# An FFT-mixing and three-way maxout kernel on one core: one more split unit per batch, x in two transfers instead of four, indexed stores moved, the last column of the head fetched through DRAM

## The chip, the cores and the metric

The kernel runs on one core of one Trainium2 chip. The metric is the device time in microseconds (us). The kernel before takes 392.08 us, the median of three runs (391.94 to 392.52). A difference of about 0.2%, 0.8 us, is what such a measurement can tell from no change.

## The reference

Two stages follow each other, all inputs and outputs in float32:

```python
# x: (8, 3072, 256);  w1, w2, w3: (256, 768);  w_out: (768, 256)
X = np.fft.fft(x, axis=1)
X = np.fft.fft(X, axis=2)
t = X.real.reshape(8 * 3072, 256)
h = np.maximum(np.maximum(t @ w1, t @ w2), t @ w3)
out = h @ w_out
```

## The kernel before

Each engine has one instruction stream, written in the order in which the Python code records the operations (`manual_schedule`). The work of one batch of x has two parts.

**Mixing.** x of a batch is fetched into `xt[b % 2]`: 96 rows apart lie on one partition, 32 partitions hold them in order (`h == 0`), 32 more hold their mirror images (`h == 1`), which is read backwards, row by row. `load_x` (L116) issues these transfers from GpSimd (POOL in the profile). `mirror`/`turn` (L123, L785) copy the upper 64 partitions from the lower ones with the columns reversed; from batch 2 on ScalarE (ACT) does it, eight pieces a batch (`turn`, units 5 to 12 two batches ahead). `s` (L392) multiplies with a 64-column table and evicts into `tb`; batch 0 turns `tb` with a VectorE (DVE) transpose (`t`, L428), later batches go through DRAM (`y`, `z`). `k` (L456) gives the cosine and sine sums `tE` and `tO` (512 columns a block, three blocks); row 0 of `tO` goes to DRAM (`vd`) and back to all partitions (`vb`, `v`, L468).

**The maxout layer.** The second FFT is folded into the weights: `g_all` holds w2 and w3 minus w1, times cosines and sines; `gd_all` is what turns the sum `tE, tO` (row block "plus") into the difference ("minus"). A batch is 18 units: unit u treats block u // 6 and hidden chunk u % 6, 512 tokens wide, plus and minus. A plain unit has six 512-column matmuls on TensorE (PE): four in `unit_plus` and two in `unit_minus`, and `unit_out` (L495) takes the maximum with one ACT and one DVE operation for each of plus and minus. A **split** unit has five: `third(g)` (L837) makes `e3` and `d3`, ACT makes `odd3`, DVE makes `even3` with the column `wcol`, and POOL adds and subtracts them (`plus3`, `minus3`, L850), two units ahead of use; `begin` (L852) and `finish` (L869) then need two matmuls plus one. All odd units from unit 7 on are split, and the even ones named in `EXTRA` (`EXTRA_LAST` in the last batch), from batch 1 on: 91 units of 144.

**The second layer.** `l2_block` (L553) multiplies `hp`, `hm` with `wout_bf`; `l2_some(10)` (L905) lets ten of its matmuls run in each unit. Plain rows are stored from SyncE (SP); the mirrored rows wait in `waiting` until `scatter(n)` (L649) issues n indexed stores from POOL, five a batch: one in units 8, 10 and 12 and two in unit 14 (L904).

What a unit's loop body (L880 to L917) records, in order: `begin(g)`, `finish(g-1)`, `third(g+2)`, `scatter`, ten matmuls of the second layer, and then the pieces that `plan` (L754) has for the unit: pieces of the next batch's mixing, transfers of x (`fetch`, L781; four a batch), and in batch 0 the rest of the preparation: `prep_first` (`next(first)`), `column` (L345, 24 one-column matmuls that make `wcol`), `prep_second`, `rows` (L727, the index column of the indexed stores, on POOL).

**The head** (L147 to L725) stands before the units: the first x in four pieces (`FIRST`, L147), ramps on POOL, tables on ACT and DVE, weights, `m.t()`, the first `k`. In the last batch `flipped` (L889) copies `tE` and `tO` backwards on POOL at unit 12, and `l2_last` (L584) ends the kernel.

Of the kernel before, what the change touches and what calls it, by code (L numbers as in the profile page):

```python
# [9 lines left out]
FP32 = mybir.dt.float32  # L10
BF16 = mybir.dt.bfloat16
# [16 lines left out]


FIRST_OF = (4, 8, 1)  # L30
EXTRA, EXTRA_LAST = (0, 4, 8), (0, 4, 8, 14)


def _parts(g):
# [10 lines left out]
def kernel(  # L45
# [9 lines left out]
    nc = tc.nc  # L55

    B, S, D = x.shape
    assert (S, D) == (3072, 256)
    DFF = moe_w1.shape[1]
    NJC = DFF // 128  # L60
# [3 lines left out]
    NS = 49  # L64
# [6 lines left out]
    consts = ctx.enter_context(tc.tile_pool(name="consts", bufs=1))  # L71
    ps_f = ctx.enter_context(tc.tile_pool(name="ps_f", bufs=3, space=bass.MemoryType.PSUM))
    d_pool = ctx.enter_context(tc.tile_pool(name="dbuf", bufs=1, space=bass.MemoryType.DRAM))
    dbs = [d_pool.tile([NS, 64 * 128], BF16, name=f"db{i}", tag=f"db{i}") for i in range(2)]
    vds = [d_pool.tile([1, NHALF], BF16, name=f"vd{i}", tag=f"vd{i}") for i in range(2)]
    t_pool = ctx.enter_context(tc.tile_pool(name="tbuf", bufs=2))

    xt = [consts.tile([128, NS * 256], BF16, name=f"xt{i}", tag=f"xt{i}") for i in range(2)]
# [17 lines left out]
    md = [md_all[:, fc * 256:(fc + 1) * 256] for fc in range(2)]  # L96
    nmd = [nmd_all[:, fc * 256:(fc + 1) * 256] for fc in range(2)]
    w1_bf = consts.tile([128, 2 * DFF], BF16, tag="w1_bf")
    w2_bf = consts.tile([128, 2 * DFF], BF16, tag="w2_bf")
    w3_bf = consts.tile([128, 2 * DFF], BF16, tag="w3_bf")  # L100
    wout_bf = consts.tile([128, NJC * 256], BF16, tag="wout_bf")
    g1t = consts.tile([128, NJC * 256], BF16, tag="g1t")
    g_all = consts.tile([128, 4 * DFF], BF16, tag="g_all")
# [6 lines left out]
    mark = consts.tile([1, 1], FP32, tag="mark")  # L110
    sgn = consts.tile([128, 1], FP32, tag="sgn")
    wcol = consts.tile([128, NJC], FP32, tag="wcol")
    dif = consts.tile([128, 1], FP32, tag="dif")
    t_mid = consts.tile([128, 2, B], BF16, tag="t_mid")

    def load_x(b, s0, s1, h):  # L116

        rows = x[b].rearrange("(a s) d -> a s d", s=96)
        lo, hi = (s0, s1) if h == 0 else (max(s0, 1), min(s1, 48))
        src = rows[:, lo:hi, :] if h == 0 else rows[:, 97 - hi:97 - lo, :][:, ::-1, :]  # L120
        return nc.gpsimd.dma_start(out=xt[b % 2][32 * h:32 * h + 32, lo:hi, :], in_=src)  # L121

    def mirror(b, s0, s1):  # L123

        t = xt[b % 2]
        fn = (nc.vector.tensor_copy, (nc.gpsimd.tensor_copy, nc.vector.tensor_copy)[s0 >= 25],
              nc.scalar.copy)[min(b, 2)]
        fn(out=t[64:128, s0:s1, 1:128], in_=t[0:64, s0:s1, 255:128:-1])  # L128
        if b < 2:
            if b == 0 and s0 < 40:  # L130
                fn = nc.scalar.copy
            fn(out=t[64:128, s0:s1, 0], in_=t[0:64, s0:s1, 128])
# [8 lines left out]
    ps_s = ps_s_cm.__enter__()  # L141

    def iota(t, pattern, base=0, cm=0):
        nc.gpsimd.iota(t, pattern, base=base, channel_multiplier=cm,
                       allow_small_or_imprecise_dtypes=True)

    FIRST = ((0, 16), (16, 32), (32, 40), (40, NS))  # L147

    pidx = gen.tile([128, 1], FP32, tag="pidx")
    iota(pidx, [[0, 1]], cm=1)  # L150
    pidx_i = gen.tile([128, 1], INT32, tag="pidx_i")
# [18 lines left out]
            iota(kvec[:, NHALF:NHALF + 1], [[0, 1]], base=0)  # L170

    dvec = gen.tile([128, 128], FP32, tag="dvec")
    for c, (s0, s1) in enumerate(FIRST):
        for h in range(2):
            load_x(0, s0, s1, h)
        if c == 0:
            iota(dvec, [[1, 128]])
        elif c < 3:
            ramp(c - 1)

    def load_w(k, j0, j1):
# [162 lines left out]

    def column():  # L345

        psc = ps_f.tile([128, 512], FP32, name="psc", tag="ps")
        for jc in range(NJC):
            for k, (table, wt) in enumerate(((md, w3_bf), (nmd, w1_bf))):
                for fc in range(2):  # L350
                    nc.tensor.matmul(psc[:, jc:jc + 1],
                                     wt[:, fc * DFF + jc * 128: fc * DFF + jc * 128 + 128],
                                     table[fc][:, 128:129],
                                     start=(k == 0 and fc == 0), stop=(k == 1 and fc == 1))
        nc.scalar.copy(out=wcol, in_=psc[:, 0:NJC])

    def prep_second():

# [290 lines left out]
    def scatter(n):  # L649

        for _ in range(min(n, len(waiting))):
            row, col, p0, p1, src = waiting.pop(0)
            stored(nc.gpsimd.indirect_dma_start(  # L653
                fours, bass.IndirectOffsetOnAxis(ap=rows_m[p0:p1, col:col + 1], axis=0),
                src, None, element_offset=256 * row), "scattered", ("scattered", "direct"))
            nc.gpsimd.memset(mark, 0.0)
# [11 lines left out]
    def warm_up(n):  # L668
        for _ in range(n):
            nc.tensor.matmul(warm, zero[:, 0:128], zero, start=True, stop=True)  # L670

    m = Mix(0)
# [8 lines left out]
    m.s(2, pool=ps_s)  # L681
    m.s(3, pool=ps_s)
    warm_up(1)
    mirror(0, *FIRST[3])
    m.s(4, pool=ps_s)
    warm_up(2)
    scal(sgn, pidx, 0.0, ALU.is_equal)
    scal(sgn, sgn, 2.0, ALU.mult, -1.0, ALU.add)
    scal(dif, sgn, 1.0, ALU.subtract)
    m.s(5, pool=ps_s, evict=dve)  # L690
    nc.scalar.activation(out=md_all, in_=vm, func=AX.Sin, scale=float(2.0 * math.pi / 256.0),
                         bias=turn[:, 0:1])
    m.s(6, pool=ps_s)
    m.t()
    warm_up(2)
# [20 lines left out]
    table(1, 512, 1024)  # L716
    m.c(1, 16)
    warm_up(1)
    m.k(0, 0, dve)
    m.k(1, 0)  # L720
    differ(0, 2, 0, 128)
    keep(psg2, 1, 2, 128, 384, dve)
    differ(0, 2, 128, 384)
# [32 lines left out]
    def at(b, unit, fn):  # L756
        plan.setdefault((b + unit // UNITS, unit % UNITS), []).append(fn)
# [23 lines left out]
    def fetch(b, k):  # L781
        half, h = divmod(k, 2)
        load_x(b, *HALVES[half], h)
# [4 lines left out]
    for (u, fn) in ((0, lambda: table(2, 512, 1024)),   # L788
                    (0, lambda: next(second)), (0, lambda: next(first)),
                    (1, lambda: m.k(1, 1)), (1, lambda: next(second)), (1, lambda: next(first)),  # L790
                    (1, lambda: table(0, 512, 1024)),
                    (2, lambda: m.v(1)), (2, lambda: m.k(0, 1)), (2, lambda: next(first)),
                    (2, lambda: next(second)), (2, lambda: next(first)), (2, lambda: table(1)),
                    (3, lambda: m.c(16, RI)), (3, lambda: m.c(0, 1)),
                    (3, lambda: table(2)), (3, lambda: table(0)),
                    (4, lambda: m.k(1, 2)), (4, lambda: m.k(0, 2)), (4, m.end),
                    (5, rows), (5, column), (5, lambda: next(second)), (6, lambda: m.v(2))):
        at(0, u, fn)

    for ch in range(4):  # L800
        at(0, (3, 3, 4, 4)[ch], lambda ch=ch: mirror(1, *CHUNKS[ch]))
        at(0, 4, lambda ch=ch: fetch(2, ch))
    for b in range(2, B):
        for ch in range(4):
            if b > 2:
                at(b - 3, (9 + (b == 3), 11, 18, 19)[ch], lambda b=b, ch=ch: fetch(b, ch))
        for ch in range(8):
            at(b - 2, 5 + ch + 3 * (b == 2), lambda b=b, ch=ch: turn(b, ch))
        at(b - 2, 13 + 3 * (b == 2), lambda b=b: mirror_first(b))
# [70 lines left out]
    for g in range(B * UNITS):  # L880
        b, u = divmod(g, UNITS)
        blk, jc = divmod(u, NJC)
        mm = mixes[b]
        last = b == B - 1 and blk == 2
        if jc == 0:
            hp = h_pool.tile([128, NJC, TOKB], BF16, name="hp", tag="hp")
            hm = h_pool.tile([128, NJC, TOKB], BF16, name="hm", tag="hm")
            if last:
                flipped = []  # L889
                for t, name in ((mm.tE, "tEr"), (mm.tO, "tOr")):  # L890
                    fl = h_pool.tile([128, TOKB], BF16, name=name, tag=name)
                    flipped.append(fl)
                    nc.gpsimd.tensor_copy(fl, t[:, 3 * TOKB - 1: 2 * TOKB - 1: -1])
        if prev is not None and is_split(prev[0]) and not is_split(g):
            finish(*prev)
            prev = None
        pses = begin(g, hp[:, jc, :])
        if prev is not None:
            finish(*prev)
        prev = (g, pses, hm[:, jc, ::-1] if last else hm[:, jc, :])  # L900
        for lead in (1, 2):
            if is_split(g + lead) and (lead == 1) == (g + lead == 7):
                third(g + lead)
        scatter({8: 1, 10: 1, 12: 1, 14: 2}.get(u, 0))  # L904
        l2_some(10)  # L905
        if b == B - 1 and u in (1, 3):
            if u == 1:
                middle = l2_mid()
            next(middle, None)
        for fn in plan.get((b, u), ()):  # L910
            fn()
        if jc == NJC - 1:
            l2_some(1000)
            if g == B * UNITS - 1:
                finish(*prev)
            l2_queue.append(l2_last(hp, hm, mm.tE, mm.tO, flipped) if last else
                            l2_block(b, blk, hp, hm, mm.tE, mm.tO))  # L917
# [32 lines left out]
```

## Time and profile before

| what | before |
|---|---|
| median of the runs | 392.08 us |
| the profiled execution | 391.42 us, span 389.3 us |
| PE busy | 376.2 us, 97% of the span |
| DVE, POOL, ACT busy | 84%, 81%, 64% |
| granted TensorE clock | 0.998 |
| DMA moved | 54.13 MB, 139 GB/s on average |

The span is the time from the first to the last instruction of the profiled execution; 2.1 us of its own time lie outside it. In an instruction's row the first two numbers are its start and length in us, and the brackets tell how long the engine was idle before it and what it waited for. A PE row of several matmuls overlaps with the next: the spacing of the starts is what a matmul costs. Rows with SPq are transfers that SP issues; their length is the time of the issue, not that of the transfer.

### The profile page before, as it was taken

How to read it: one execution, taken by the hardware profiler on the slowest of the kernel's cores; microseconds unless marked ns; L12 is line 12 of the kernel's file. 1: busy time of each engine (PE TensorE's matmuls, PEld its weight loads, DVE VectorE, ACT ScalarE, POOL GpSimd, SP SyncE). 2: the span in 40 equal slices, each digit the busy share in tenths (PEclk: the TensorE clock that was granted, in tenths of full speed). 3: DMA queues.
4: the chain of work that ended last, by engine and by line, in shares of the span. 5: the costliest groups of instructions: out<-in, count | busy, mean ns of one | idle time of the engine just before them, and what ended most of it. 6: DMA issues, size and time to landing. Idle time of an engine off the chain costs nothing.

```text
span 389.3 us, 8092 instructions
## 1 busy us (share of the span) xinstructions
PE 376.2 (97%) x2817; PEld 236.2 (61%) x2817; DVE 327.7 (84%) x552; ACT 248.4 (64%) x453; POOL 314.3 (81%) x363
## 2 busy tenths in 40 slices
PE   6699999999999999999999999999999999999985
PEld 2355566566665666566665666656665666666654
DVE  7788797799797988899797988989887997999972
ACT  6877789567856696567856687567866346434420
POOL 9983576879898898879898898879787887769881
PEclk9999999999999999999999999999999999999999
DMA  7999764585747666475938657575423544212226
GB/s 113 184 183 160 163 145 118 112 168 161 178 141 130 172 176 154 111 128 186 189 120 149 169 151 176 125 128 185 113 94 93 149 138 139 70 31 80 85 89 206
DMA packets 52263, 54.13 MB, mean 139 GB/s; under 512 B 26547, under 2 KB 45009, under 8 KB 51367
## 3 DMA queue, kind: packets, MB, share of 16 engines
q0 software_dynamic: 20272, 26.45, 34.4%
q1 hardware_dynamic: 31418, 26.58, 25.0%
q10 hardware_dynamic: 532, 0.59, 0.5%
q8 instruction: 22, 0.36, 0.3%
q14 instruction: 19, 0.16, 0.1%
HBM read 36.95 MB, written 30.81 MB: 174 GB/s over the span
## 4 chain that ended last, share of the span: by engine, by line
PE 87%; POOL 4%; DVE 4%; DMA 2%; ACT 1%; issue 1%; DVEq 0%; POOLq 0%
PE po L549 30%; PE pse L492 10%; PE pse L860 5%; PE pse L485 5%; PE pse L486 5%; PE d L843 5%; PE e L841 5%; PE pse L861 5%; PE po L572 5%; PE ps L461 3%; PE ps L396 3%; PE pl L565 2%; DMA xt<-in_x_dram 2%; POOL xt L121 1%; POOL plus L850 1%
## 5 line engine op out<-in xcount | busy, mean ns | idle before, releaser
L850 POOL TENSOR_TENSOR plus<-even,odd 128x512 bf16<-128x512 f32 x91 | 115.7, 1271 | 55.4 <-DVE even L846 44.1
L850 POOL TENSOR_TENSOR minus<-even,odd 128x512 bf16<-128x512 f32 x91 | 115.5, 1269 | 0.0
L845 ACT ACTIVATE odd<-d 128x512 f32<-128x512 f32 x91 | 54.4, 598 | 55.8 <-PE d L843 41.9
L862 DVE SCALAR_TENSOR_TENSOR hp<-pse,plus 128x512 bf16<-128x512 f32 x91 | 62.6, 688 | 32.2 <-PE pse L861 27.9
L549 PE MATMUL po<-wout_bf,hp 128*128 128x256 bf16 x576 | 86.1, 273 | 0.0
L498 ACT ACTIVATE stmp<-pse 128x512 bf16<-128x512 f32 x106 | 63.2, 600 | 24.2 <-PE pse L486 11.2
L549 PE MATMUL po<-wout_bf,hm 128*128 128x256 bf16 x576 | 78.6, 273 | 0.0
L549 PEld LDWEIGHTS <-hp 128*128 128x128 bf16 x576 | 56.3, 98 | 26.2
L492 PE MATMUL pse<-tO,gd_all 128*128 128x512 bf16 x197 | 66.1, 380 | 1.3 <-DVE hp L862 1.3
L846 DVE SCALAR_TENSOR_TENSOR even<-vb,wcol,e 128x512 f32<-128x512 bf16 x91 | 67.1, 737 | 0.0
L549 PEld LDWEIGHTS <-hm 128*128 128x128 bf16 x576 | 56.3, 98 | 16.4
L874 DVE SCALAR_TENSOR_TENSOR hm<-pse,minus 128x512 bf16<-128x512 f32 x91 | 61.9, 680 | 0.4
L499 DVE TENSOR_TENSOR hp<-pse,stmp 128x512 bf16<-128x512 f32 x53 | 36.4, 686 | 8.8 <-ACT stmp L498 4.2
L499 DVE TENSOR_TENSOR hm<-pse,stmp 128x512 bf16<-128x512 f32 x53 | 36.5, 689 | 6.7 <-ACT stmp L498 4.3
L485 PE MATMUL pse<-tE,g_all 128*128 128x512 bf16 x106 | 40.2, 379 | 0.8 <-DVE tE L463 0.4
L577 DVE TENSOR_TENSOR kq<-po,even 128x512 f32<-128x512 f32 x60 | 40.9, 682 | 0.0
L128 ACT COPY xt<-xt 64x762 bf16<-64x762 bf16 (+1 forms) x48 | 39.8, 838 | 1.0
L486 PE MATMUL pse<-tO,g_all 128*128 128x512 bf16 x106 | 40.2, 379 | 0.0
L572 PE MATMUL po<-gw,tO 128*128 128x512 bf16 x92 | 34.9, 379 | 0.0
L860 PE MATMUL pse<-tE,g_all 128*128 128x512 bf16 x91 | 34.6, 380 | 0.1
L653 POOL DMA_INDIRECT out_dram<-kq,rows_m x29 | 29.0, 1000 | 6.8 <-issue 5.7
L841 PE MATMUL e<-tE,g_all 128*128 128x512 bf16 x91 | 34.5, 379 | 0.0
(173 smaller groups left out, 511.7 us busy)
## 6 DMA issues: line engine op xcount, KB each, us to landing
xt<-in_x_dram POOLq DMA_DIRECT2D x14, 384.0 KB
db<-tb SPq DMA_DIRECT2D x21, 192.0 KB
out_dram<-obuf SPq DMA_DIRECT2D x8, 384.0 KB
out_dram<-kq SPq DMA_DIRECT2D x8, 384.0 KB
vb<-vd SPq DMA_DIRECT2D x23, 128.0 KB
xt<-in_x_dram POOLq DMA_DIRECT2D x7, 400.0 KB
xt<-in_x_dram POOLq DMA_DIRECT2D x7, 368.0 KB
out_dram<-kq SPq DMA_DIRECT2D x7, 288.0 KB
```

The costliest lines, as they stand in the source:

```text
L485: nc.tensor.matmul(pse[:, 0:n], g_all[:, jc, 2 * i, :], te, start=True, stop=False)
L486: nc.tensor.matmul(pse[:, 0:n], g_all[:, jc, 2 * i + 1, :], to, start=False, stop=True)
L492: nc.tensor.matmul(pse, gd_all[:, jc, i, :], to, start=False, stop=True, skip_group_check=True)
L498: nc.scalar.activation(out=stmp[:, 0:n], in_=pses[0][:, 0:n], func=AX.Relu)
L499: nc.vector.tensor_tensor(out=dst, in0=src3, in1=stmp[:, 0:n], op=ALU.max)
L549: nc.tensor.matmul(po, hcols(jc), wout_bf[:, jc * 256:(jc + 1) * 256], start=False, stop=(jc == NJC - 1), skip_group_check=True)
L572: nc.tensor.matmul(po, to[:, cp], gw[:, 256:768], start=True, stop=True)
L845: nc.scalar.activation(out=odd3, in_=d3, func=AX.Copy, scale=-0.5)
L846: nc.vector.scalar_tensor_tensor(out=even3, in0=vb, scalar=wcol[:, jc:jc + 1], in1=e3, op0=ALU.mult, op1=ALU.add)
L850: nc.gpsimd.tensor_tensor(out=dst, in0=even3, in1=odd3, op=op)
L862: nc.vector.scalar_tensor_tensor(out=dst, in0=pse2, scalar=0.0, in1=sums[g][0], op0=ALU.max, op1=ALU.max)
L874: nc.vector.scalar_tensor_tensor(out=dst, in0=pses[0], scalar=0.0, in1=sums.pop(g)[1], op0=ALU.max, op1=ALU.max)
```

## The change

- **Split units.** `EXTRA` gets unit 12; in the last batch unit 12 takes the place of unit 14.
- **Indexed stores.** One in units 0, 4, 8, 12 and 14, in the last batch also one in unit 16.
- **x.** From batch 3 on a batch comes in two transfers, `h == 0` at unit 13 and `h == 1` at unit 18 three batches ahead, instead of four at units 9 (10), 11, 18 and 19. Batches 0 to 2 keep theirs, but for the first.
- **The first x.** The transfer of its first 16 rows is issued before the first `iota`s on POOL; the last nine rows come as five and four.
- **Head evictions.** The evictions of `s(5)`, `k(0, 0)` and `k(1, 0)` are halved between DVE and ACT; `md_all` is made on ACT before the half of `s(5)`, and three small DVE operations (`sgn`, `dif`) go ahead of the last mirrors.
- **The column.** `wcol` is no longer computed: row 0 of `g_all[:, :, 3, :]` is written to DRAM from SP (unit 3), read back as a column of 2-byte elements (`column_read`, unit 4, SP), and cast on POOL (`column_done`, unit 5, ahead of `rows`).

```diff
-EXTRA, EXTRA_LAST = (0, 4, 8), (0, 4, 8, 14)
+PACE, PACE_LAST = {0: 1, 4: 1, 8: 1, 12: 1, 14: 1}, {0: 1, 4: 1, 8: 1, 12: 1, 14: 1, 16: 1}
+EXTRA, EXTRA_LAST = (0, 4, 8, 12), (0, 4, 8, 12)
...
+    wd = d_pool.tile([1, DFF], BF16, name="wd", tag="wd")
...
+    wcol_b = consts.tile([128, NJC], BF16, tag="wcol_b")
...
-    FIRST = ((0, 16), (16, 32), (32, 40), (40, NS))
+    FIRST = ((0, 16), (16, 32), (32, 40), (40, 45), (45, NS))
+    def load_first(c):
+        for h in range(2):
+            load_x(0, *FIRST[c], h)
+    load_first(0)
     pidx = gen.tile([128, 1], FP32, tag="pidx")
...
-    for c, (s0, s1) in enumerate(FIRST):
-        for h in range(2):
-            load_x(0, s0, s1, h)
-        if c == 0:
-            iota(dvec, [[1, 128]])
-        elif c < 3:
+    iota(dvec, [[1, 128]])
+    for c in range(1, 5):
+        load_first(c)
+        if c < 3:
             ramp(c - 1)
...
     def column():
-        psc = ps_f.tile([128, 512], FP32, name="psc", tag="ps")
...
-        nc.scalar.copy(out=wcol, in_=psc[:, 0:NJC])
+        nc.sync.dma_start(out=wd.rearrange("o (c j) -> o c j", j=128), in_=g_all[0:1, :, 3, :])
+    def column_read():
+        nc.sync.dma_start(out=wcol_b, in_=wd.rearrange("o (c j) -> j (o c)", j=128))
+    def column_done():
+        nc.gpsimd.tensor_copy(wcol, wcol_b)
...
     warm_up(1)
-    mirror(0, *FIRST[3])
-    m.s(4, pool=ps_s)
-    warm_up(2)
     scal(sgn, pidx, 0.0, ALU.is_equal)
...
-    m.s(5, pool=ps_s, evict=dve)
+    mirror(0, *FIRST[3])
+    mirror(0, *FIRST[4])
+    m.s(4, pool=ps_s)
+    warm_up(2)
     nc.scalar.activation(out=md_all, in_=vm, func=AX.Sin, scale=float(2.0 * math.pi / 256.0),
                          bias=turn[:, 0:1])
+    def halves(out, in_):
+        n = out.shape[-1] // 2
+        if len(out.shape) == 4:
+            n = 2
+            dve(out=out[:, :, 0:n, :], in_=in_[:, :, 0:n, :])
+            nc.scalar.copy(out=out[:, :, n:, :], in_=in_[:, :, n:, :])
+        else:
+            dve(out=out[:, 0:n], in_=in_[:, 0:n])
+            nc.scalar.copy(out=out[:, n:], in_=in_[:, n:])
+    m.s(5, pool=ps_s, evict=halves)
...
-    m.k(0, 0, dve)
-    m.k(1, 0)
+    m.k(0, 0, halves)
+    m.k(1, 0, halves)
...
-                    (5, rows), (5, column), (5, lambda: next(second)), (6, lambda: m.v(2))):
+                    (3, column), (4, column_read), (5, column_done), (5, rows), (5, lambda: next(second)), (6, lambda: m.v(2))):
...
-        for ch in range(4):
+        for h in range(2):
             if b > 2:
-                at(b - 3, (9 + (b == 3), 11, 18, 19)[ch], lambda b=b, ch=ch: fetch(b, ch))
+                at(b - 3, (13, 18)[h], lambda b=b, h=h: load_x(b, 0, NS, h))
...
-        scatter({8: 1, 10: 1, 12: 1, 14: 2}.get(u, 0))
+        scatter((PACE if b < B - 1 else PACE_LAST).get(u, 0))
```

More of the change, by code (lines that the diff above doesn't have):

```diff
@@ L345, in column @@
     def column():
-        psc = ps_f.tile([128, 512], FP32, name="psc", tag="ps")
[L348 to L354, printed above, removed]
-        nc.scalar.copy(out=wcol, in_=psc[:, 0:NJC])
+        nc.sync.dma_start(out=wd.rearrange("o (c j) -> o c j", j=128), in_=g_all[0:1, :, 3, :])
[3 more added lines that the diff above has]
+        nc.gpsimd.tensor_copy(wcol, wcol_b)
     def prep_second():
```

## The prediction

> **What bounds the kernel now.** First the page's part 1 and its chain that ended last: TensorE (PE) is busy nearly all the time, and the chain runs through it.
>
> ```profile
> PE 376.2 (97%) x2817; PEld 236.2 (61%) x2817; DVE 327.7 (84%) x552; ACT 248.4 (64%) x453; POOL 314.3 (81%) x363
> PE 87%; POOL 4%; DVE 4%; DMA 2%; ACT 1%; issue 1%; DVEq 0%; POOLq 0%
> ```
>
> Then the windows, to see where the other 13.1 us of the span lie. Columns: length, then busy time and count of PE, PEld, DVE, ACT, POOL, then clock, DMA share, GB/s. First the head from 20 us on, then one whole batch (44.3 us, as every batch from 1 to 6), then the last units.
>
> ```profile
> 20.00:50.00 30.00, 28.82 (x220) 16.54 (x220) 24.58 (x44) 22.56 (x45) 17.89 (x32) 1.00 0.97 169
> 157.40:201.70 44.30, 44.30 (x334) 28.00 (x332) 38.35 (x61) 30.91 (x55) 38.20 (x41) 1.00 0.65 153
> 366.00:378.00 12.00, 10.66 (x72) 6.82 (x71) 9.26 (x16) 3.23 (x6) 11.15 (x13) 1.00 0.20 67
> ```
>
> In the batches PE never stops, at a granted clock of 1.00: only fewer matmuls shorten them. A 512-column matmul costs 0.217 us there (the spacing of the starts; its row's 0.38 us overlaps the next). At the end PE stands still for 1.34 us, and the chain of waits says why:
>
> ```profile
> 369.13 0.89 POOL out_dram L653
> 370.03 0.08 POOL mark L656
> 370.11 1.25 POOL plus L850
> ...
> 372.77 1.12 POOL out_dram L653
> ...
> 374.19 0.98 POOL out_dram L653
> ...
> 375.26 1.25 POOL plus L850
> 376.52 0.02 issue
> 376.54 0.70 DVE hp L862
> ```
>
> Three indexed stores stand on POOL ahead of the sums of split units 15 and 17, which PE then waits for (0.76 us at 372.14, 0.59 us at 377.28 in the timeline). In the head, a chain of small steps leads to the first split unit's sum; SP's and POOL's timeline rows there matter for the column:
>
> ```profile
> 33.39 0.23 SPq L466 DMA_DIRECT2D vd<-tO  x1
> 35.79 1.38 SPq L418 DMA_DIRECT2D db<-tb  x2
> 38.13 1.41 SPq L470 DMA_DIRECT2D vb<-vd  x1
> 41.46 1.26 POOL L850 TENSOR_TENSOR plus<-even,odd 128x512 bf16<-128x512 f32 x1 [8.35 <-DVE even L846]
> ```
>
> **Unit 12 split.** It drops one matmul, 0.217 us, in batches 1 to 6: 6 x 0.217 = 1.30 us off the path. In batch 7 it changes places with unit 14: no matmul gained.
>
> What it adds must stay hidden. DVE: 0.74 us for `even3`, on 38.35 of 44.3. ACT: 0.60 less. POOL: two sums, 2.5 us from start to end of the pair, on 38.2. POOL saves on x: four issues cost 0.56 + 0.77 + 0.56 + 0.80 = 2.69 us a batch. The `h == 0` issue takes 0.56 whatever its length (32 long runs); the reversed one takes 0.59 for 256 rows and 0.77 for 768, so about 1.0 for 1504 (bounds 0.77, one of today's, and 1.57, two). So 1.6 instead of 2.7, and POOL gets 38.2 + 2.5 - 1.1 = 39.6 of 44.1 us, 90%. On average it fits. Locally: units 7, 8, 9 are three splits in a row today, and POOL takes them as they come, its pairs starting at 172.87, 175.34 and 178.03, the last 0.20 us after waiting for DVE. With unit 12 there are 11, 12, 13: sums recorded in units 9, 10, 11, which start at 179.02, 181.41 and 183.36 in this batch. A sum is ready 2.8 us after its unit's start; 11's pair ends 5.3 us after, at 184.3, which is when 12's is ready; 12's ends at 186.8, and 13's, ready at 186.2, starts 0.7 us late. Its `plus` has 3.0 us to spare today before PE needs the DVE result made from it (the least in the batch is 1.3, unit 9; the most 4.7). The stores moved to units 0, 4, 8, 12, 14 follow units that record no even sum, and find POOL between triples: after 13's pair ends at 189.3, a store (1.05 + 0.3 us) ends at 190.7, where 15's sums, ready at 191.0, start on time. I take no stall: 1.30 us in full.
>
> **The last units.** Before: sums for 13, 14, 15, 17 and three stores between units 12 and 15. Now 12's are recorded at 10, the stores sit at 12, 14 and 16, and 14 has none. Run through POOL: 13's pair ends at 365.8, the two flipped copies (0.6 each) at 367.0, the store at 368.3; 15's `plus` ends at 369.6, against a need at about 370.6; a store until 372.1, 17's pair at once, with the third store behind it. Both stalls go: 0.76 + 0.59 = 1.35 us. What is late next is PE itself, with 6.7 us of matmuls and stores to the end that nothing here touches.
>
> **The head.** The transfers of the first x run back to back and bound `m.t()`: DVE waits 0.97 us for the last nine rows at 13.37. Issuing the first ones 0.67 us earlier (the iotas cost 0.84 to 1.51) moves them all by about that, and the last mirror gets shorter. But ACT is full: its casts end at 13.7, `md_all` takes 0.74, then come half of `s(5)` (about 0.36 from the 0.57 of 512 columns and the fixed part in 0.27 for 128) and `s(6)` at 0.27: the transpose can start some 0.4 us earlier (15.31 before). ACT's copy into `yb` at 19.16 and PE's wait for `x0` behind POOL's later `u` (POOL is 1.2 us later there, by one more pair of issues and what waits for free slots) leave 0.1 to 0.2 of it; halving `tE` and `tO` gives another 0.15 to 0.3, since unit 0's second matmul needs `tO` (20.59). Together 0.3 (bounds 0 and 0.6). The later POOL brings the mirror of batch 1's second piece to about 29.6, where PE reads it at 29.7: just covered; if not, 0.3 is lost.
>
> `column`'s 24 matmuls hold PE from 35.06 to 35.66, in the chain ahead of `psw`: 0.6 us less. So up to 0.9 us is gained by the first split unit, unless the column's new way is later. It is: SP writes `wd` at about 29.2, after `g_all` is complete at 29.0. Today's small writes of that stretch, `vd<-tO` at 24.70 and 33.39, let their readers go at 29.05 and 38.13, 4.35 and 4.74 us later, so `column_read` goes at 33.7. Landing: at best as a small write, 4.5 us, 38.2; at worst as `db<-tb`, issued at 35.79 and landed at 43.2, 7.4 us, 41.1. The nearest row is the 128-piece `vb<-vd` over all engines, issued at 29.05 and landed at 34.2: 5.2 us, so 39.2 with the longer issue. Then POOL: the cast (0.19, as `rows_m`'s), `rows`, which is queued behind it (1.46 us, 31.66 to 33.12), the first `plus`. With 0.2 for the signals it can start at 39.2 + 1.85 = 41.05 instead of 41.46: a gain of 0.4. The bounds give 40.05, where the head's own 0.9 is the limit, and 42.95, a loss of 1.5. DVE's `even3` waits for the cast too, but sooner. From there on PE carries the shift unchanged.
>
> [...]
>
> **x.** One transfer of 1504 rows instead of two. ACT first needs it in unit 5, its wait marked at 127.1 in batch 2. The `h == 1` issue moves to about 117.5; today's 736 rows issued at 120.06 land at 125.1, and 768 rows more take 2.0 us at the 382 rows per us of its middle: 117.5 + 5.0 + 2.0 = 124.5, 125.5 behind the store's packets: 1.6 us early. Cost nothing; without that cover, rival 3.
>
> **Sum.** 1.30 + 1.35 + 0.4 = 3.05. The profiled execution of 391.42 us would take 388.4; the median of the runs lies 0.66 above it, so 392.08 - 3.05 = 389.0.
>
> **Rivals.**
> 1. The column is in time, the head gives 0.9: 392.08 - 2.65 - 0.9 = 388.5. For it: between 30.5 and 33 us few packets run, and the first x's traffic ends earlier. Against: both `vd` rows. [...]
> 2. The column is late as `db<-tb`, or later with its 768 pieces of two bytes: head +1.5, so 392.08 - 2.65 + 1.5 = 390.9. All is lost when it lands at 41.46 + 2.65 - 1.85 = 42.3. [...]
> 3. Slower: x's single reversed transfer lands after ACT's need in unit 5. ACT then holds `odd3` and the sums, PE stalls. It decides from 1.6 us later on. If the 1504 rows, sharing the engines with `db<-tb` (first packets at 124.0), land 3 us later than worked out, ACT waits 1.4 us in each of five batches: 389.0 + 7 = 396. Against: at 382 rows per us they are through by then.
> 4. POOL at 90% falls behind: no gain from unit 12, and 0.5 us in six batches: 389.0 + 1.3 + 3 = 393.3. Against: the triple above.
>
> That the change doesn't do what it says is out: the changed program's order has 97 pairs of sums and no `psc`.
>
> **How the numbers follow.** Forecast 0.52; rival 1 0.20; 2 0.16; 3 0.07; 4 0.05. Measurable is 0.8 us (0.2%). Faster takes the forecast, rival 1 and half of 2, 0.80; the rest of 2 is mostly "same", 0.07; slower 0.13. The range goes from rival 1 with the head's upper bound (388.2) to rival 2 with half of unit 12 lost (391.5), 0.2 more at both ends for the scatter of the runs; 3, 4 and the tail of 2 stay out.
>
> **What would show it.** A batch of 44.08 us with PE busy throughout; no PE gap over 0.2 us after 360; `plus` first starting at 40 to 41.5; the wait in front of POOL's `wcol` cast ending near 39. Wrong: waits of ACT on x in unit 5, PE gaps at units 13 to 15, a first `plus` after 42.

## The result, and the profile after

The changed kernel takes 394.18 us (median of six runs, 393.62 to 394.75), the kernel before 392.01 on the same chip (six runs, 391.67 to 392.59): ratio 1.0054, 95% interval 1.0041 to 1.0066, 2.2 us slower. Forecast were 389.0, with 388.0 to 391.7 as the range. The profiled execution took 394.04 us, its span 392.0. One thing the times below need: in some executions of one and the same kernel the granted TensorE clock falls to 0.50 for 3.41 us or more, in others it does not, so a median and a profile of one kernel can differ (col_old: median 389.6, the profiled execution, with such a fall, 391.54).

The page's first part and its chain. PE's share is smaller than before, and two DMAs have come into the chain:

```profile
PE 374.5 (96%) x2738; PEld 237.2 (61%) x2787; DVE 333.6 (85%) x561; ACT 246.3 (63%) x448; POOL 325.5 (83%) x368
PE 89%; DMA 3%; POOL 2%; ACT 2%; DVE 2%; issue 2%; POOLq 0%; DVEq 0%
```

The same windows as before (columns: length, busy time and count of PE, PEld, DVE, ACT, POOL, clock, DMA share, GB/s): the head, one batch, the last units.

```profile
20.00:50.00 30.00, 25.59 (x184) 14.42 (x187) 21.52 (x39) 19.44 (x43) 16.43 (x35) 0.96 1.05 166
163.80:207.87 44.07, 43.64 (x326) 27.92 (x331) 38.87 (x62) 30.53 (x54) 39.54 (x40) 1.00 0.67 154
366.00:378.00 12.00, 11.95 (x81) 7.80 (x80) 11.11 (x19) 5.25 (x9) 11.64 (x13) 1.00 0.22 60
```

The batch came out as forecast: 44.07 us, POOL at 39.54 (PE's 43.64 are of 326 matmuls, where steady_only's same window below has 333: seven records are missing). At the end no PE gap over 0.1 us is left after 352. The loss is in the head, where PE does 25.59 us of work in 30 instead of 28.82, with a clock of 0.96 instead of 1.00. The column's chain there, from SP's and POOL's timeline:

```profile
32.62 0.78 SPq L353 DMA_DIRECT2D wd<-g_all  x1
39.31 0.40 SPq L357 DMA_DIRECT2D wcol_b<-wd  x1
44.98 0.19 POOL L361 CAST wcol<-wcol_b 128x6 f32<-128x6 bf16 x1 [11.25 <-DMA wcol_b<-wd]
46.55 1.26 POOL L868 TENSOR_TENSOR plus<-even,odd 128x512 bf16<-128x512 f32 x1
```

The first `plus` starts at 46.55 instead of 41.46. PE stands still for 2.69 us around it (45.90 to 48.59), until VectorE has made `hp` from that sum. From the waits between 40 and 53 us, with the total, the times and the longest:

```profile
PE pse L498 <- DVE hp L880: 2.7, 1, 2.7
DVE even L864 <- POOL wcol L361: 2.2, 1, 2.2
```

How the delay against before runs through the span, measured at the same instruction of both traces: unit 0's first matmul +2.62 (20.36 to 22.98), first `plus` +5.09, the second layer's very first addition +5.09 and its second +6.26, the first addition of batch 1 +6.39; then 0.217 less in each batch down to +5.10 in the last; +3.15 at PE's last matmul, +2.70 at the end of the span.

### The profile page after: what moved, and what is told of

Same layout as the page of the kernel before. It is cut to its first block, busy times and chain, and to the rows that moved or that the text cites. A ratio compares the mean times of both kernels' runs of the same rounds, so it can differ in the third digit from the quotient of the medians.

```text
span 392.0 us, 8001 instructions
## 1 busy us (share of the span) xinstructions
PE 374.5 (96%) x2738; PEld 237.2 (61%) x2787; DVE 333.6 (85%) x561; ACT 246.3 (63%) x448; POOL 325.5 (83%) x368
## 4 chain that ended last, share of the span: by engine, by line
PE 89%; DMA 3%; POOL 2%; ACT 2%; DVE 2%; issue 2%; POOLq 0%; DVEq 0%
PE po L555 32%; PE pse L498 11%; PE e L859 5%; PE d L861 5%; PE pse L878 5%; PE po L578 5%; PE pse L879 5%; PE pse L492 5%; PE pse L491 5%; PE ps L467 3%; PE ps L402 3%; PE pl L571 3%; PE psg L314 2%; DMA wd<-g_all 2%; DMA wcol_b<-wd 1%
## 5 line engine op out<-in xcount | busy, mean ns | idle before, releaser
L868 POOL TENSOR_TENSOR plus<-even,odd 128x512 bf16<-128x512 f32 x97 | 123.2, 1270 | 36.8 <-DVE even L864 31.2
L868 POOL TENSOR_TENSOR minus<-even,odd 128x512 bf16<-128x512 f32 x97 | 123.2, 1270 | 0.0
L880 DVE SCALAR_TENSOR_TENSOR hp<-pse,plus 128x512 bf16<-128x512 f32 x97 | 66.7, 688 | 28.9 <-PE pse L879 19.6
L864 DVE SCALAR_TENSOR_TENSOR even<-vb,wcol,e 128x512 f32<-128x512 bf16 x97 | 71.6, 738 | 2.2 <-POOL wcol L361 2.2
L504 ACT ACTIVATE stmp<-pse 128x512 bf16<-128x512 f32 x94 | 56.0, 600 | 25.7 <-PE pse L492 13.2
L892 DVE SCALAR_TENSOR_TENSOR hm<-pse,minus 128x512 bf16<-128x512 f32 x97 | 66.1, 682 | 0.4
L505 DVE TENSOR_TENSOR hp<-pse,stmp 128x512 bf16<-128x512 f32 x47 | 32.3, 688 | 8.3 <-ACT stmp L504 4.6
L861 PE MATMUL d<-tO,gd_all 128*128 128x512 bf16 x97 | 36.8, 379 | 0.1
L575 ACT COPY even<-pl 128x512 f32<-128x512 f32 x46 | 26.8, 583 | 11.4 <-DVE kq L583 7.8
L491 PE MATMUL pse<-tE,g_all 128*128 128x512 bf16 x85 | 32.7, 385 | 1.1 <-ACT tE L708 0.6
```

The costliest lines, as they stand in the source:

```text
L504: nc.scalar.activation(out=stmp[:, 0:n], in_=pses[0][:, 0:n], func=AX.Relu)
L505: nc.vector.tensor_tensor(out=dst, in0=src3, in1=stmp[:, 0:n], op=ALU.max)
L861: nc.tensor.matmul(d3, gd_all[:, jc, 1, :], to, start=True, stop=True)
L864: nc.vector.scalar_tensor_tensor(out=even3, in0=vb, scalar=wcol[:, jc:jc + 1], in1=e3, op0=ALU.mult, op1=ALU.add)
L868: nc.gpsimd.tensor_tensor(out=dst, in0=even3, in1=odd3, op=op)
L880: nc.vector.scalar_tensor_tensor(out=dst, in0=pse2, scalar=0.0, in1=sums[g][0], op0=ALU.max, op1=ALU.max)
```

## The experiments

The kernels' marks, in us from the span's start, are read from the one profiled execution of each. "s" is the start of the last matmul group of the first x, "turn" VectorE's transposition, "k" the first `k` matmul, "unit 0" its first matmul. The time is the median of the runs; col_quiet and col_runs12 were run once, h_load and h_pieces twice. The runs are from several chips, on which the kernel before takes 392.01 to 392.51, so medians of two kernels compare to some 0.5 us; the ratios are each against before on the same chip.

| kernel | s | turn | k | unit 0 | first plus | time |
|---|---|---|---|---|---|---|
| before | 14.06 | 15.31 | 19.13 | 20.36 | 41.46 | 392.0 |
| after | 15.07 | 16.54 | 21.62 | 22.98 | 46.55 | 394.18 |
| steady_only | 14.45 | 15.70 | 19.53 | 20.76 | 41.87 | 389.03 |
| x_old | 14.11 | 15.36 | 19.17 | 20.40 | 41.51 | 388.98 |
| col_old | 15.19 | 16.66 | 21.67 | 23.02 | 44.44 | 389.6 |
| head_old | 14.68 | 15.93 | 19.78 | 21.01 | 44.04 | 391.26 |
| warm | 15.00 | 16.47 | 20.29 | 21.66 | 45.39 | 393.56 |
| col_quiet | 14.46 | 15.72 | 19.55 | 20.77 | 41.51 | 400.15 |
| col_runs12 | 14.55 | 15.80 | 19.63 | 20.86 | 43.85 | 390.28 |
| h_load | 14.06 | 15.31 | 19.12 | 20.35 | 41.46 | 388.66 |
| h_pieces | 13.95 | 15.20 | 19.54 | 20.75 | 42.53 | 389.26 |
| h_halves | 14.04 | 16.36 | 21.25 | 22.61 | 44.03 | 390.72 |
| h_order | 14.44 | 15.93 | 20.97 | 22.19 | 43.28 | 389.34 |
| h_lp | 13.54 | 14.94 | 19.65 | 20.86 | 42.59 | 389.74 |
| h_lpo | 15.08 | 16.33 | 20.14 | 21.36 | 42.47 | 389.86 |

Where code of the head is the same (before, steady_only, x_old, col_quiet, col_runs12, head_old), s lies at 14.06 to 14.68 and unit 0 at 20.36 to 21.01: that is the scatter of one execution against another. A mark inside this scatter tells nothing of an edit.

**steady_only.** Head (its loads, pieces, evictions and order) and column as before; unit 12, the stores and x's two transfers stay.

```diff
-        nc.sync.dma_start(out=wd.rearrange("o (c j) -> o c j", j=128), in_=g_all[0:1, :, 3, :])
+        psc = ps_f.tile([128, 512], FP32, name="psc", tag="ps")
...
-                    (3, column), (4, column_read), (5, column_done), (5, rows), (5, lambda: next(second)), (6, lambda: m.v(2))):
+                    (5, rows), (5, column), (5, lambda: next(second)), (6, lambda: m.v(2))):
...
-    FIRST = ((0, 16), (16, 32), (32, 40), (40, 45), (45, NS))
+    FIRST = ((0, 16), (16, 32), (32, 40), (40, NS))
...
-    m.s(5, pool=ps_s, evict=halves)
+    m.s(5, pool=ps_s, evict=dve)
...
```

> The head and the column as in the kernel before; unit 12 split, the stores moved and x in two transfers as in the changed one. Theory (the loss is all in the head and the column; behind them the gains came as worked out): comparing the DVE additions of the second layer one by one, the changed kernel is 6.39 us late at batch 1, 5.09 at the end of batch 7's second block, 2.89 at the last: 1.30 and 2.2 gained. So 392.0 - 3.5 = 388.5, within 0.5, and a batch of 44.07 us. Rival (those gains are only the recovery of a late start, which waits less on POOL and x): 390.5 or more, and a batch of 44.2 to 44.3.

Measured: 389.03 (388.80 to 389.51; before 392.32 on this chip), ratio 0.9911, interval 0.9893 to 0.9930. The steady part is worth 3.3 us on this chip: the prediction had 1.30 + 1.35 = 2.65, the expectation 3.5. The rival (390.5 or more) fell, and this version beats both kernels. Its windows of one batch and of the end:

```profile
157.50:201.57 44.07, 44.07 (x333) 27.91 (x331) 38.88 (x62) 30.52 (x54) 39.58 (x41) 1.00 0.67 153
366.00:378.00 12.00, 12.00 (x90) 8.54 (x89) 9.96 (x16) 3.46 (x6) 9.41 (x13) 1.00 0.30 94
```

**col_old.** The kernel after with the 24 matmuls for the column.

```diff
-        nc.sync.dma_start(out=wd.rearrange("o (c j) -> o c j", j=128), in_=g_all[0:1, :, 3, :])
+        psc = ps_f.tile([128, 512], FP32, name="psc", tag="ps")
...
-                    (3, column), (4, column_read), (5, column_done), (5, rows), (5, lambda: next(second)), (6, lambda: m.v(2))):
+                    (5, rows), (5, column), (5, lambda: next(second)), (6, lambda: m.v(2))):
```

> The changed kernel with the column from 24 matmuls again; the new head stays. Theory: unit 0 still starts 2.6 us late (at 23.0), but the 2.5 us that the column's transfers add by the first sums and the 1.3 us of slow TensorE clock behind that wait go: 392.0 + 2.6 - 3.5 = 391.1. Rival (the column's transfers only fill time that the late head leaves anyway): within 0.8 of the changed kernel's 394.2.

Measured: 389.6 (389.44 to 391.54), ratio 0.9925, interval 0.9904 to 0.9946. That is 1.5 us less than the theory's 391.1. By the medians the new column costs the kernel after 4.6 us. Four runs lie at 389.44 to 389.82 with a mean clock of 0.997 to 1.000. The profiled one, at 391.54 and 0.995, has a clock of 0.50 from 17.21 to 20.62 and unit 0 at 23.02, as after. So the new head costs about 0.6 us against steady_only without a clock drop and 2.5 with one; the theory had counted the drop in every run.

**head_old.** The kernel after with the head of before; the column goes via DRAM.

```diff
-    FIRST = ((0, 16), (16, 32), (32, 40), (40, 45), (45, NS))
+    FIRST = ((0, 16), (16, 32), (32, 40), (40, NS))
...
-    m.s(5, pool=ps_s, evict=halves)
+    m.s(5, pool=ps_s, evict=dve)
...
```

> The changed kernel with the whole head of before; the column still goes through DRAM. Theory: unit 0 starts at 20.4; the column is written at about 29.2, and with the 6.7 and 5.5 us that the two transfers took it lands near 41.4, the first plus starts near 43.3 instead of 41.5, 1.8 us late, and TensorE's wait may cost it clock for up to 1.3: 392.0 + 1.8 - 3.5 = 390.3, with the clock 391.6. Rival (the transfers take 4.5 and 5.2 us when the head is on time, as predicted): plus at about 41, 388.1 to 388.5.

Measured: 391.26 (390.47 to 393.94), ratio 0.9988, interval 0.9968 to 1.0008: the column eats most of what the steady part gains. Six of the ten runs lie at 390.47 to 391.39 with a mean clock of 0.997 to 1.000, so the column costs about 1.8 us by itself, as the theory had it; the run at 0.996 takes 392.36 and the three at 0.992 to 0.993 take 392.73 to 393.94. From its timeline:

```profile
29.69 0.78 SPq L353 DMA_DIRECT2D wd<-g_all  x1
35.12 0.39 SPq L357 DMA_DIRECT2D wcol_b<-wd  x1
42.48 0.19 POOL L361 CAST wcol<-wcol_b 128x6 f32<-128x6 bf16 x1 [10.36 <-DMA wcol_b<-wd]
```

**col_quiet.** head_old, with batch 2's x fetched in unit 7.

```diff
-        at(0, 4, lambda ch=ch: fetch(2, ch))
+        at(0, 7, lambda ch=ch: fetch(2, ch))
```

> The kernel of head_old (head as before, column via DRAM) with the x of batch 2 fetched three units later, so that it is not on the queues beside the column's write and read. In head_old the write took 5.43 us from issue to its end and the read 7.3. Theory: x's traffic makes part of these times, and write and read together take 8 to 10 us against 12.7, the first plus 41.5 to 43 against 44.04. Rival: the 768 pieces of 2 bytes make the time, and both together stay above 11.5 us.

Measured, in the same rows, and the DMA share while the column is on its way (0.15 and 0.14; in head_old 0.94 and 1.30 over the same two stretches):

```profile
29.51 0.78 SPq L353 DMA_DIRECT2D wd<-g_all  x1
33.80 0.24 SPq L472 DMA_DIRECT2D vd<-tO  x1
34.09 0.39 SPq L357 DMA_DIRECT2D wcol_b<-wd  x1
36.93 0.19 POOL L361 CAST wcol<-wcol_b 128x6 f32<-128x6 bf16 x1 [8.70 <-DMA wcol_b<-wd]
```

```profile
29.50:34.00 4.50, 3.80 (x36) 1.93 (x35) 3.84 (x7) 4.50 (x11) 0.00 (x0) 1.00 0.15 33
34.00:37.00 3.00, 3.00 (x22) 1.80 (x22) 2.94 (x8) 1.53 (x4) 0.07 (x1) 1.00 0.14 1
```

Write and read together take 7.42 us instead of 12.79, less than the theory's 8 to 10: x's traffic is the cause. Even the 4.58 us from write to read are not the write's own time: SP issues `vd<-tO` at 33.80, ahead of the read, and the trace marks no wait for `wd` behind it, where SP waits 0.8 us for `wd` in head_old and 2.9 in after. The packet records agree: the write's six pieces of 256 bytes move 1.4 to 1.5 us behind its issue here and 4.3 to 4.9 us behind it in head_old (5.9 to 6.3 in after). The first `plus` comes at 41.51, 20.74 us behind unit 0 against 21.11 in steady_only: here the column is in time. The 0.37 us less are part of the 0.6 forecast for its 24 matmuls, but x's later fetch may have a part in them. The whole takes 400.15, since x is now late. In the waits from 40 to 62 us:

```profile
ACT xt L131 <- DMA xt<-in_x_dram: 12.2, 1, 12.2
...
PE pse L491 <- ACT stmp L504: 9.9, 1, 9.9
```

**col_runs12.** head_old, with the column read back in another order.

```diff
-        nc.sync.dma_start(out=wcol_b, in_=wd.rearrange("o (c j) -> j (o c)", j=128))
+        nc.sync.dma_start(out=wcol_b, in_=wd.rearrange("o (j c) -> j (o c)", c=NJC))
```

> The kernel of head_old with the column read back in another order, as 128 runs of 12 bytes in place of 768 pieces of 2 bytes; the column's values are so in the wrong places. In head_old the write took 5.43 us and the read 7.3. Theory (the pieces' number makes little of it beside x's traffic): the read takes 5 to 7 us and the first plus comes at 42.5 to 44.1 against 44.04. Rival: the pieces make it, and the read takes under 4.5 us, with the first plus at 40.5 to 42.

Measured, in one run: write issued at 29.54, read at 36.46, cast at 42.29: 6.92 + 5.83 = 12.75 us against 12.79, first `plus` at 43.85. Six times fewer pieces change nothing, and the theory's numbers held.

**warm.** The kernel after with twelve more matmuls of zeros in the head.

```diff
     m.s(4, pool=ps_s)
-    warm_up(2)
+    warm_up(9)
...
     m.t()
-    warm_up(2)
+    warm_up(7)
```

> The changed kernel with 12 more idle matmuls on zeros in the two gaps of TensorE in the head (seven behind s(4), five behind s(6)). [...]

Measured: 393.56 (390.97 to 395.76), ratio 1.0020, interval 0.9996 to 1.0043. In after PE is idle for 1.50 us ahead of 15.07 and for 1.00 us ahead of 17.18, and its clock is 0.50 from 17.44 to 20.85; the twelve matmuls go into these two gaps. The windows of 3.41 us, first in after (two rows in the head, two around the column's gap), then in warm; the clock is the third number from the end:

```profile
14.03:17.44 3.41, 1.36 (x12) 0.71 (x13) 2.31 (x5) 2.18 (x6) 3.41 (x11) 1.00 0.99 120
17.44:20.85 3.41, 3.41 (x26) 2.74 (x24) 2.82 (x1) 1.82 (x6) 3.41 (x8) 0.50 1.14 159
...
44.75:48.16 3.41, 1.10 (x9) 0.78 (x8) 1.06 (x2) 0.65 (x2) 2.96 (x11) 1.00 0.74 164
48.16:51.57 3.41, 2.98 (x10) 1.32 (x10) 3.41 (x6) 1.42 (x2) 2.84 (x5) 0.50 0.42 136
```

```profile
14.03:17.44 3.41, 3.41 (x23) 1.56 (x22) 1.58 (x3) 2.27 (x6) 3.41 (x9) 1.00 1.01 121
17.44:20.85 3.41, 3.20 (x45) 2.58 (x43) 2.87 (x2) 2.63 (x8) 3.41 (x8) 1.00 1.06 151
```

With PE kept busy the head's clock stays at 1.00 in this execution, and unit 0 comes 1.32 us sooner (21.66 for 22.98), nearly all of it between turn and k: 3.82 us for 5.08. That the clock makes these 1.26 us does not rest on warm alone: with the same x and the same small operations ahead, col_old takes 5.01 with a drop and h_lpo 3.81 without one. h_lpo also shows that a head without idle matmuls can escape the drop, so one profile of warm does not prove that they prevent it. The median gains 0.6 us (1.3 by the ratios): the column's gap remains, with PE busy for 0.62 of the 3.41 us ahead of 48.03, and the clock is 0.50 from 48.03 to 51.44. One execution in which the mean clock is 0.999 took 390.97.

**The head's edits one by one**, each on steady_only.

h_load:

```diff
+    load_first(0)
     pidx = gen.tile([128, 1], FP32, tag="pidx")
...
-    load_first(0)
```

h_pieces:

```diff
-    FIRST = ((0, 16), (16, 32), (32, 40), (40, NS))
+    FIRST = ((0, 16), (16, 32), (32, 40), (40, 45), (45, NS))
...
+    mirror(0, *FIRST[4])
```

h_halves:

```diff
-    m.s(5, pool=ps_s, evict=dve)
+    m.s(5, pool=ps_s, evict=halves)
...
-    m.k(0, 0, dve)
-    m.k(1, 0)
+    m.k(0, 0, halves)
+    m.k(1, 0, halves)
```

h_order:

```diff
-    mirror(0, *FIRST[3])
-    m.s(4, pool=ps_s)
-    warm_up(2)
     scal(sgn, pidx, 0.0, ALU.is_equal)
...
+    mirror(0, *FIRST[3])
+    m.s(4, pool=ps_s)
+    warm_up(2)
+    nc.scalar.activation(out=md_all, in_=vm, func=AX.Sin, scale=float(2.0 * math.pi / 256.0),
+                         bias=turn[:, 0:1])
```

> The kernel of steady_only (head and column as before) with one edit: the first load is issued ahead of the iotas. In the profile after, the first iota ended later for it (POOL's sequencer issues the load first) and VectorE's serial chain of table work ran 0.6 us later, while x landed 0.8 us earlier. Theory: VectorE bounds the head, so the earlier x is worth nothing and unit 0's first matmul, at 20.76 in steady_only, comes at 21.0 to 21.4. Rival: x bounds the head, and unit 0 comes at 20.0 to 20.5. Time 389.0 to 389.7 by the theory, 388.3 to 388.8 by the rival.

> The kernel of steady_only with one edit: the first batch's x in five pieces in place of four, with the mirror of the fifth. POOL issues one more pair of transfers, so its ramp, memset and later issues come a microsecond later and run beside VectorE's last mirrors. Theory: those mirrors are stretched as in the profile after (0.55 and 0.16 us there became 0.81, 0.87 and 0.45), and the last s matmuls start at 14.8 to 15.3 against 14.45, unit 0 at 21.0 to 21.6 against 20.76. Rival: the stretch comes from the late start of VectorE's chain alone (the early load), and the smaller last piece brings the s matmuls to 14.0 to 14.3 and unit 0 to 20.3 to 20.6. Time 389.3 to 389.9 by the theory, 388.6 to 388.9 by the rival.

> The kernel of steady_only with one edit: the three evictions of the head, of s and of the two of k, go half to VectorE and half to ScalarE. Theory: the ScalarE half waits for the VectorE half, so each step is as long as both together: from the last s matmuls to the transpose 1.4 to 1.5 us against 1.17, from the first k matmul to unit 0 1.30 to 1.40 against 1.23, and unit 0 at 21.0 to 21.3 against 20.76. Rival (the prediction's): both halves run at once, and unit 0 comes at 20.3 to 20.6. Time 389.3 to 389.6, or 388.6 to 388.9.

> The kernel of steady_only with one edit: the small sign operations of VectorE ahead of the last mirror, the sine table ahead of the eviction of s. Theory: VectorE has an idle stretch ahead of the last mirror, so its part is free, and with the sine table off the end of the eviction unit 0 comes within 0.2 us of 20.76. Rival: the small operations push the last mirror, and unit 0 comes at 21.1 to 21.6. Time within 0.4 of 389.0, or 389.4 to 389.9.

(The expectations count "the transpose" 0.08 us ahead of the row's start.) h_load: unit 0 at 20.35, 388.66 (two runs). These are the rival's numbers, but before and x_old have 20.36 and 20.40 with the old order, so the edit moves nothing beyond the scatter and decides for neither. h_pieces: s at 13.95, so the rival's sooner s held, but unit 0 came at 20.75 and the first `plus` 0.66 later than in steady_only, 389.26: PE waits 0.8 us there for POOL's mirror of batch 1's second piece. h_order: s at 14.44, so its part on VectorE is free; the profiled execution had a clock of 0.50 from 13.50 to 20.33, which brings unit 0 to 22.19 and that run to 390.42, while the other two took 389.15 and 389.34. h_halves: 390.72 (390.04 to 392.02), ratio 0.9950, worse than both expectations. Its profiled execution (391.29) had a clock of 0.50 from 13.21 to 20.04, so its marks behind s hold the clock's part too; the four runs at 0.998 to 1.000 still took 390.04 to 390.86. From ScalarE's and VectorE's timeline there:

```profile
15.18 0.37 ACT L702 CAST tb<-ps 128x256 bf16<-128x256 f32 x1 [1.37 <-DVE tb L701]
15.45 0.72 ACT L708 ACTIVATE md_all<-vm,turn 128x512 bf16<-128x512 int32 x1
16.07 0.25 ACT L417 CAST tb<-ps 64x128 bf16<-64x128 f32 x1
```

```profile
14.72 0.42 DVE L701 CAST tb<-ps 128x256 bf16<-128x256 f32 x1 [0.25 <-PE ps L402]
16.36 3.71 DVE L435 STREAM_TRANSPOSE yb<-tb 128x2048 uint32<-128x2048 uint32 x1 [1.21 <-ACT tb L417]
```

The ScalarE half starts only after the VectorE half has ended; here the sine table, which in this kernel stands behind that half, pushes the last eviction and with it the transposition. From k to unit 0 it took 1.36 us against 1.23 (expected 1.30 to 1.40).

**x_old.** steady_only with the four transfers of before.

```diff
-        for h in range(2):
+        for ch in range(4):
             if b > 2:
-                at(b - 3, (13, 18)[h], lambda b=b, h=h: load_x(b, 0, NS, h))
+                at(b - 3, (9 + (b == 3), 11, 18, 19)[ch], lambda b=b, ch=ch: fetch(b, ch))
```

> The kernel of steady_only with the four x transfers a batch of before in place of the two. Theory: no engine waits for x either way, so the time is within 0.4 us of steady_only's 389.03. Rival: the two large transfers relieve POOL's issue and carry part of the gain, and the time is 389.8 to 390.5.

Measured: 388.98 (388.42 to 389.44) against 389.03, ratio 0.9918 against 0.9911. x's two transfers are worth nothing, and cost nothing.

**h_lp and h_lpo.** None of the four edits alone brings s to 15.07. So two and three together: h_lp is steady_only with the early load and the five pieces, h_lpo has the small operations ahead as well (the head of after but for the halves).

> The kernel of steady_only with the early first load and the five pieces together. Each of the two alone left the last s matmuls at 14.06 (early load) and 13.95 us (five pieces), against 14.45 in steady_only and 15.07 in the profile after. Theory: together they put VectorE's last mirrors, late by the early load, under GpSimd's ramps and issues, late by the fifth piece; the mirrors are stretched as after, and the last s matmuls start at 14.8 to 15.3, the transposition at 16.0 to 16.5. Rival: the pairing is harmless, the last s matmuls start at 13.9 to 14.5, and the small sign operations ahead of the mirrors make the lost time after. Time 389.3 to 390.0 by the theory, 388.5 to 389.1 by the rival.

> The kernel of col_old without its halves: early load, five pieces, sign operations and sine table moved ahead, the three evictions on one engine as before. Theory: the last s matmuls start at 14.9 to 15.3 as in col_old (15.19), and with one engine's eviction the transposition starts 1.2 us behind them in place of 1.47, at 16.1 to 16.5. The TensorE clock may or may not fall to 0.50 behind it (it is decided from execution to execution): without, unit 0 comes at 21.2 to 21.6, with it at 22.4 to 22.8. Rival: the halves were needed for the stretch, and the last s matmuls start before 14.6. Time 389.4 to 390.0 at full clock by the theory, under 389.2 by the rival.

h_lp: s at 13.54, sooner than in any other; the theory of the pair fell. h_lpo: s at 15.08 as after, and 21.36 for unit 0 at full clock: the halves are not needed for it. Its four runs took 388.88 to 390.77, the two at 0.998 and 1.000 of the clock 389.21 and 388.88, less than the theory's 389.4 to 390.0. VectorE's rows, first after, then h_lp:

```profile
12.56 0.15 DVE L223 TENSOR_SCALAR sgn<-pidx 128x1 f32<-128x1 f32 x1
12.75 0.15 DVE L223 TENSOR_SCALAR sgn<-sgn 128x1 f32<-128x1 f32 x1
12.94 0.15 DVE L223 TENSOR_SCALAR dif<-sgn 128x1 f32<-128x1 f32 x1
13.10 0.69 DVE L131 COPY xt<-xt 64x635 bf16<-64x635 bf16 x1
13.72 0.81 DVE L135 COPY xt<-xt 64x5 bf16<-64x5 bf16 x1
13.78 0.87 DVE L131 COPY xt<-xt 64x508 bf16<-64x508 bf16 x1
14.57 0.45 DVE L135 COPY xt<-xt 64x4 bf16<-64x4 bf16 x1
```

```profile
12.99 0.19 DVE L135 COPY xt<-xt 64x5 bf16<-64x5 bf16 x1
13.06 0.28 DVE L131 COPY xt<-xt 64x508 bf16<-64x508 bf16 x1
13.26 0.23 DVE L135 COPY xt<-xt 64x4 bf16<-64x4 bf16 x1
```

The three small operations start where the mirrors would run and hold them for 0.54 us, and then the mirrors themselves are slow: 0.81, 0.87 and 0.45 us instead of 0.19, 0.28 and 0.23. In after and h_lpo GpSimd's ramps (14.12 on) lie beside the later ones, in h_lp the ramps begin at 14.91, when the mirrors are done. But the ramps can't be all of it: the first slow mirror (13.10, 0.69 us, against 0.35 in h_pieces) ends before they begin. GpSimd's three issues of `w_bf` beside it are slow as well, 3.01 us from 12.01 against 2.12 from 12.80 in h_lp. What slows both was not tried by itself and stays open. Yet h_lp's whole took 389.74: what it gains at s (0.9 us against steady_only, 0.5 to 1.1 against the scatter) is lost again, at two places that its waits name (15 to 20 us, 29 to 33 us), both behind POOL's later issues. The second is the mirror that the prediction called just covered, at a price of 0.3 if not:

```profile
PE psg L314 <- DMA w_bf<-in_moe_w_dram: 1.1, 1, 1.1
```

```profile
PE ps L402 <- POOL xt L135: 0.8, 1, 0.8
```

## Why the prediction was wrong

**Held.** Unit 12 split: 6.39 to 5.10 us of delay over batches 1 to 6, 1.29 against 1.30. POOL at 39.5 us of 44.07 (worked out: 39.6) keeps up, so rival 4 fell; ScalarE does not wait for x, so rival 3 fell, and x_old shows the edit to be neutral. The end: both stalls are gone. From the same addition of the last batch to PE's last matmul it takes 28.55 us instead of 30.50, 1.95 against the 1.35 forecast. The 0.6 on top lies in how the stalls were read. The prediction took their idle times, 0.76 and 0.59 us, which count from the end of the matmul row before, and that end overlaps with the next start; by the spacing of the starts they cost more. In before:

```profile
370.56 0.82 PE L549 MATMUL po<-wout_bf,hp 128*128 128x256 bf16 x6
372.14 0.38 PE L492 MATMUL pse<-tO,gd_all 128*128 128x512 bf16 x1 [0.76 <-DVE hp L862]
```

Six matmuls of 256 columns cost 0.65 us at 0.217 for 512, so the next could start at 371.21 and starts 0.93 later. The second stall costs 0.75 by the same sum, and two shorter delays, ahead of 373.99 and 374.58, 0.12 and 0.14: together 1.94. In steady_only, which has the same 206 matmuls there, none of the four is left.

**Failed: the head.** "Together 0.3 (bounds 0 and 0.6)" sooner; it was 2.62 later at unit 0, outside the bounds. By rows of after against before: s 1.01 later, s to transposition 1.47 for 1.25, from there to k 5.08 for 3.82, k to unit 0 1.36 for 1.23; 1.01 + 0.22 + 1.26 + 0.13 = 2.62. Three steps of the reasoning failed. "The transfers of the first x ... bound `m.t()`": they came sooner (VectorE waits for no transfer of x in after; h_lp's s shows what that could give), but VectorE's queue bounded it once the small operations stood ahead of the mirrors; the prediction gave that move no price, though the 0.97 us of idle time that could have covered it were what the earlier x removes. The halves were taken as running side by side; they run one behind the other:

```profile
15.98 0.37 ACT L705 CAST tb<-ps 128x256 bf16<-128x256 f32 x1 [1.23 <-DVE tb L704]
```

VectorE's half, on the same tile `ps`, ran from 15.52 to 15.94. The halves share the tile `tb` too, and which of the two tiles makes the wait is not shown. And the sum had no term for the clock, which was 1.00 in every row of before that the prediction shows.

**Failed: the column.** The prediction's own sign of being wrong, a first `plus` after 42, came at 46.55. Three terms failed. The write was issued at 32.62 instead of 29.2, mostly because the head was late. It took 6.69 us, not 4.5 (5.43 in head_old, 6.92 in col_runs12); the read took 5.67 to POOL's cast, close to the 5.5 worked out, but 7.36 in head_old. I had taken both from the transfers of before around 24 to 38 us and did not ask what else the new ones would meet; col_quiet, with at most 4.58 for the write and 2.84 for the read, shows that batch 2's x is what they meet. So rival 2 was the true case of the column (a landing like `db<-tb`, 390.9; head_old measured 391.26), and on top of it came the head. That the two numbers lie so close is partly luck: the steady part gained 3.3 and not 2.65 us, and the column lost more than the rival's 1.5. The 2-byte pieces, which I had named as a risk, are not the cause (col_runs12). The 0.2 us for the signals in the sum's 1.85 was an assumption that no row shows; from the cast's start to the first `plus` it took 1.57 us in after and 1.56 in head_old.

**Failed: no price for a gap on PE.** The column's wait of 2.69 us (45.90 to 48.59) is followed by a clock of 0.50 until 51.57, 3.41 us from 48.16 on: from the first second-layer addition to the fifth it takes 14.43 us instead of 13.26, 1.17 us more. In the profiled execution of head_old, where PE waits 2.24 us for the column and the clock stays at 1.00, nothing is added there. The sum of the head: 2.62 at unit 0, 2.47 from there to the first `plus` (23.57 for 21.10; 0.3 of it without the new column, as col_old's 21.42 shows), 1.17 by the clock, 0.13 that steady_only and head_old show at the same place: 6.39. Minus 1.29 for unit 12, 1.95 at the end, and 0.45 between PE's last matmul and the span's end (4.15 for 4.61 us, which scatters from 4.15 to 5.39 over the kernels): 2.70, the difference of the spans.

## What to carry to other kernels

A step moved through DRAM is priced by the traffic it will meet at its new place, not by the rows of like transfers at other times: beside x's fetch the same write and read took 12.8 us, without it 7.4 at most. An idle stretch can be spent only once: here the earlier x and the operations moved into the gap both used the same 0.97 us. A gap on PE can cost twice: in after 2.69 us of waiting and then 1.17 us in the 3.41 us at a clock of 0.50; in head_old's profile a wait of 2.24 us, with the clock at 1.00, cost nothing more. Try the steady part of a change apart from the one-off parts: steady_only keeps 3.3 us that the whole change lost.

## What the runs showed of the hardware that I had not expected

While the kernels have work, the granted clock falls to 0.50 for 3.41, 6.83 or 10.24 us: 3.41 in after (17.44 to 20.85 and 48.16 to 51.57), col_old (17.21 to 20.62) and warm (48.03 to 51.44), 6.83 in h_halves (13.21 to 20.04) and h_order (13.50 to 20.33), 10.24 in col_quiet (52.76 to 63.00). In the 3.41 us ahead of these seven drops PE was busy for 1.36 and 1.10 us (after), 1.12 (col_old), 0.62 (warm), 1.81 (h_halves), 1.85 (h_order) and 0.00 (col_quiet); col_old's and warm's are summed from windows of 0.2 us. Two windows of h_order:

```profile
10.09:13.50 3.41, 1.85 (x10) 0.49 (x9) 3.03 (x9) 3.19 (x8) 3.41 (x8) 1.00 1.45 188
13.50:16.91 3.41, 2.70 (x15) 1.32 (x15) 2.56 (x4) 2.29 (x5) 3.41 (x9) 0.50 1.28 170
```

Executions of one kernel differ: h_order's profiled one has a mean clock of 0.988 and takes 390.42, another has 1.000 and takes 389.15. After's mean clock was 0.989 to 0.991 in five of six runs, about what two drops of 3.41 us give (6.82 x 0.5 / 392 = 0.009), and 0.996 in the fastest. A mean alone does not tell where a drop is: before's 0.998 comes from the last us (0.50 from 387.38 on; the last matmul ends at 384.71).

PE's busy time in the 3.41 us ahead does not tell it either. In before PE is busy for 1.59 us from 7.50 to 10.91, in head_old for 1.48 us in the first of these windows, and the clock stays at 1.00 behind both:

```profile
44.16:47.57 3.41, 1.48 (x9) 0.85 (x9) 2.23 (x4) 0.61 (x2) 2.85 (x5) 1.00 0.46 102
47.57:50.98 3.41, 3.29 (x24) 2.12 (x23) 3.17 (x6) 2.36 (x4) 2.35 (x2) 1.00 0.56 177
```

Both are less than the 1.81 and 1.85 us ahead of the drops in h_halves and h_order. What decides whether the clock falls is not shown.
